# New lists for a set-attention kernel: loads after the first batch may be issued by either of two engines

## The chip, the cores and the metric

The kernel runs on one core of a Trainium2 chip. A core has five engines that work at the same time: TensorE (PE, matrix products, with a path of its own for loading weights, PEld), VectorE (DVE), ScalarE (ACT), GpSimd (POOL) and SyncE (SP), and sixteen DMA engines that move data between device memory and the core. The metric is the device time of the whole program in microseconds (us). Before the change it was 273.87 us, the median of three runs (273.7 to 274.29).

## What is computed

There are four batches of 12800 rows of 128 channels. First an attention through 32 inducing rows: the inducing rows attend to x, which gives h (32 rows), and then every row of x attends to h. On the result a gated product follows: a causal convolution of five taps over the rows, put through a sigmoid, times a linear map of the same rows, times an output matrix.

```python
def mab(q, kv):
    s = scale * (q @ kv.transpose(0, 2, 1))
    s = s - s.max(-1, keepdims=True)
    a = np.exp(s)
    a /= a.sum(-1, keepdims=True) + 1e-09
    return a @ kv
h = mab(I, x)                 # 32 inducing rows attend to 12800 rows of x
x = mab(x, h)                 # every row of x attends to the 32 rows of h
for k in range(5):
    gate_pre += conv_w[k] * xp[:, k:k + S, :]
out = (1 / (1 + exp(-gate_pre)) * (x @ w_val)) @ w_out
```

## The kernel before

The rows of a batch are cut into seven or eight chunks of up to 480 columns on each of four strips. Two copies of x are loaded: `xt` (channels on the partitions, `load_xt`, line 244), which both attentions score, and `xk` (rows on the partitions, `load_xk`, line 274), which the first attention sums. For most chunks of batch 0 there is no load of `xk`: PE transposes `xt` instead (line 298) and ACT or DVE copies the result (line 199). A full load is close to 1 MB.

The stages of a chunk are: scores of the inducing rows (`s1`, line 320) and their maximum (line 349), the exponential (ACT, line 366), the weighted sum h (`h`, line 398). When a batch has all its h, a short chain of small steps joins the groups (lines 415 to 466, DVE and PE), then come the scores of every row against h (`s2`, line 611) with a softmax over DVE, POOL and ACT (lines 617 to 691) that leaves `P`, the weights in two halves of float16. The matrix `W` (line 540, many small products with the identity, `ident`) folds h with the value matrix and the taps. For a block of rows the gate is PE's line 705 and the linear map line 714, ACT's sigmoid line 764, the product line 774 on DVE, its two halves lines 792 and 797, the output product line 823 and the store line 849.

Nothing of the order is left to a scheduler while the kernel runs. `Plan.op` records 1534 steps and numbers them. The list `SEQ` gives all of them in one order, and each engine follows it for its own steps; `BANKS` gives each accumulator one of four banks of PSUM; `ELSE` puts a step on another engine than its usual one. A transfer is issued by an engine's own instruction stream, so it stands in line behind that engine's earlier instructions. In the kernel before, loads of batches 0 and 1 are SP's (of batch 1 `ELSE` may put one on ACT) and those of batches 2 and 3 are ACT's.

Each buffer (`BUFS`: 11 of `xt`, 4 of `xk`) is taken by a new load once all readers of its former content are done. Transfers also share eight semaphores in turn: a transfer waits until an earlier one that used its semaphore has landed, in the lists of instructions the waits on `DMAHW0` to `DMAHW7`.

Of the kernel before, what the change touches and what calls it, by code (L numbers as in the profile page):

```python
# [26 lines left out]
SP = 1024.0  # L27
# [63 lines left out]
def tile_kernel(ctx: ExitStack, tc: tile.TileContext, xt, xk, indT_in, w64, out):  # L91
# [18 lines left out]
    op = plan.op  # L110
# [101 lines left out]
    blocks = []  # L212

    def load(dur, fn, new, use=(), b=0):
        return op("SP" if b < 2 else "ACT", dur, fn, [], new, use, dma=(dur, "load"), alt=dict(SP=dur, ACT=dur) if b == 1 else None)
# [663 lines left out]
    def ws():  # L879
        nonlocal iw  # L880
        iw = weights(load(0.66, f_wload, [("tg", "w", 0)]))
# [216 lines left out]
```

## Time and profile before

| | before |
|---|---|
| median of three runs | 273.87 us |
| the profiled execution | 274.29 us |
| its span in the trace | 272.3 us |
| PE busy in the span | 262.5 us, 96% |
| DVE, POOL, ACT busy | 229.0, 206.2, 198.2 us |
| moved by DMA | 75.49 MB, mean 277 GB/s |

The profiled execution took 274.29 us, of which 272.3 are the span between its first and last recorded work; 2.0 us lie around it. PE is the engine that is nearly always busy, so the time is PE's work and the moments at which PE stands still. DMA is nearly full in the first sixth of the run and has room later: over the span it moves 277 GB/s, in the first 45 us some 415.

The program itself is also read by DMA. The profile has a queue for it, with packets of about 16.5 KB. Where it says that an engine waited for "issue", the engine waited for nothing that the profile shows: no semaphore of another engine's work released it.

### The profile page before, as it was taken

What the parts mean: (1) busy time and instruction counts of PE and PEld (TensorE: products, weight loads), DVE (VectorE), ACT (ScalarE), POOL (GpSimd) and SP (SyncE); (2) the same over time, 40 slices, a digit from 0 to 9 for tenths busy, and PEclk for the clock granted to TensorE, in tenths of its full rate; (3) what the DMA queues carried; (4) which work ended last, traced back from release to release, by engine and by line L of the source; (5) the groups of instructions that cost most, each with busy time, mean ns of one, the idle gap of its engine ahead of it and who ended that gap; (6) DMA issues with size and microseconds to landing.
All of it is one profiled execution on the core that took longest, in us unless ns stands there. A gap on an engine that the chain in (4) does not pass through costs nothing.

```text
span 272.3 us, 11127 instructions
## 1 busy us (share of the span) xinstructions
PE 262.5 (96%) x4705; PEld 145.2 (53%) x4705; DVE 229.0 (84%) x539; ACT 198.2 (73%) x300; POOL 206.2 (76%) x233
## 2 busy tenths in 40 slices
PE   8999888999999999999999999999999999999984
PEld 3668436655665565485444455574544445444542
DVE  1678888899789999988899999879979999888842
ACT  2456157777877895877789788787788887777793
POOL 2000366878868979869899988888999999998960
PEclk9999999999999999999999999999999999999999
DMA  7999998898899989989999999734253323434547
GB/s 272 425 415 420 414 394 348 296 339 332 237 400 370 389 276 375 346 243 385 300 307 368 327 338 353 258 111 151 97 191 139 120 110 132 172 142 163 184 164 285
DMA packets 35377, 75.49 MB, mean 277 GB/s; under 512 B 2816, under 2 KB 26752, under 8 KB 35328
## 3 DMA queue, kind: packets, MB, share of 16 engines
q10 hardware_dynamic: 19520, 36.96, 39.1%
q1 hardware_dynamic: 15808, 37.82, 36.5%
q8 instruction: 37, 0.61, 0.9%
q14 instruction: 12, 0.10, 0.1%
HBM read 48.56 MB, written 26.21 MB: 275 GB/s over the span
## 4 chain that ended last, share of the span: by engine, by line
PE 95%; DVE 1%; issue 1%; ACT 1%; DVEq 0%; ACTq 0%
PE g L705 31%; PE a L823 24%; PE a L398 9%; PE a L611 8%; PE a L320 8%; PE a L714 6%; PE g L298 3%; PE a L859 1%; PE a L540 1%; PE a L813 1%; PE a L465 1%; ACT xk L199 0%; PE a L484 0%; PE a L349 0%; PE a L566 0%
## 5 line engine op out<-in xcount | busy, mean ns | idle before, releaser
L797 POOL TENSOR_TENSOR gl<-tg,gh 128x960 f16<-128x960 f32 (+4 forms) x54 | 101.2, 1878 | 12.3 <-ACT gh L792 6.5
L705 PE MATMUL g<-P,W 32*128 32x480 f16 (+4 forms) x1740 | 103.1, 345 | 1.3 <-issue 1.3
L705 PEld LDWEIGHTS <-W 32*128 32x128 f16 x1740 | 51.3, 92 | 42.7 <-issue 12.3
L774 DVE SCALAR_TENSOR_TENSOR tg<-tg,a 128x480 f32<-128x480 f32 (+4 forms) x116 | 65.4, 602 | 7.1 <-PE a L714 4.5
L792 ACT CAST gh<-tg 128x960 f16<-128x960 f32 (+4 forms) x54 | 50.1, 929 | 17.2 <-DVE tg L774 14.9
L823 PE MATMUL a<-gh,wo 128*32 128x480 f16 (+6 forms) x618 | 61.4, 348 | 0.8 <-DVE tg L774 0.7
L764 ACT ACTIVATE tg<-g,gsc 128x960 f32<-128x960 f32 (+4 forms) x58 | 55.7, 993 | 4.5 <-PE g L705 3.8
L823 PEld LDWEIGHTS <-wo 128*32 128x32 f16 (+1 forms) x939 | 35.2, 97 | 35.2 <-issue 14.2
L714 PE MATMUL a<-P,W 32*128 32x480 f16 (+4 forms) x348 | 41.9, 345 | 0.1
L836 DVE TENSOR_SCALAR os<-a,osc 128x480 f32<-128x480 f32 (+4 forms) x59 | 37.8, 661 | 4.8 <-PE a L823 3.8
L823 PE MATMUL a<-gl,wo 128*32 128x480 f16 (+6 forms) x309 | 41.5, 347 | 0.0
L838 ACT ACTIVATE os<-a,osc 128x448 f32<-128x448 f32 (+3 forms) x49 | 30.7, 638 | 5.9 <-PE a L823 3.2
L691 POOL TENSOR_TENSOR P<-pt,P 128x480 f16<-128x480 f32 (+4 forms) x29 | 30.1, 1037 | 4.1 <-ACT P L684 3.8
L398 PE MATMUL a<-xk,et 128*32 128x129 f32 x800 | 29.3, 274 | 0.2 <-issue 0.2
L628 POOL TENSOR_TENSOR e<-e,m 128x480 f32<-128x480 f32 (+4 forms) x29 | 27.2, 940 | 2.8 <-DVE m L622 1.9
L398 PEld LDWEIGHTS a<-xk,et 128*32 128x32 f32 x800 | 25.4, 110 | 6.4 <-issue 2.9
L611 PE MATMUL a<-xt,hT 128*32 128x480 f32 (+4 forms) x232 | 27.7, 541 | 0.1
L673 POOL TENSOR_TENSOR e<-e,z 128x480 f32<-128x480 f32 (+4 forms) x29 | 27.1, 937 | 0.6 <-DVE z L666 0.2
L320 PE MATMUL a<-xt,indT 128*32 128x480 f32 (+4 forms) x232 | 27.4, 544 | 0.2 <-DVE bt L172 0.2
L328 DVE TENSOR_SCALAR_CACHE_REDUCE ss<-a 128x480 f32<-128x480 f32 (+4 forms) x29 | 17.5, 605 | 7.2 <-PE a L320 6.8
L366 ACT ACTIVATE ss<-ss,ng 128x480 f32<-128x480 f32 (+4 forms) x29 | 18.0, 656 | 5.2 <-DVE ng L356 5.1
L684 ACT CAST P<-pt 128x480 f16<-128x480 f32 (+4 forms) x29 | 16.2, 561 | 7.5 <-DVE pt L679 7.0
(112 smaller groups left out, 285.4 us busy)
## 6 DMA issues: line engine op xcount, KB each, us to landing
xt<-in_xt_dram ACTq DMA_DIRECT2D x10, 960.0 KB, 7.3
out_dram<-os SPq DMA_DIRECT2D x35, 240.0 KB, 2.6
xk<-in_xk_dram ACTq DMA_DIRECT2D x8, 967.5 KB, 7.7
xt<-in_xt_dram SPq DMA_DIRECT2D x7, 960.0 KB, 10.2
out_dram<-os SPq DMA_DIRECT2D x28, 224.0 KB, 3.3
xk<-in_xk_dram ACTq DMA_DIRECT2D x6, 903.0 KB, 8.0
xk<-in_xk_dram SPq DMA_DIRECT2D x5, 903.0 KB, 12.5
out_dram<-os ACTq DMA_DIRECT2D x17, 240.0 KB, 3.7
```

The costliest lines, as they stand in the source:

```text
L320: T.matmul(s[32 * r:32 * r + 32, :n], c_["indT"], x[:, o:o + n // 32, r, :], start=True, stop=True)
L398: T.matmul(t[32 * s:32 * s + 32, :P + 1], st["et", b, c][:, 32 * i:32 * i + 32], st["xk", b, q][:, m + i, :], start=j < R, stop=j >= n - R)
L611: T.matmul(s[32 * r:32 * r + 32, :n], st["hT", b], x[:, m:m + nb, r, :], start=True, stop=True)
L705: T.matmul(st[f"g{r // 2}", b, c][:, r % 2, :n], st["W", b][q, w, k, :], st[("P1", "P2")[e]][q, o:o + n], start=u == 0, stop=u == len(taps ...
L714: T.matmul(st["a", "v", b, c, r][:, :n], st["W", b][q, w, TAPS, :], st[("P1", "P2")[e]][q, o:o + n], start=u == 0, stop=u == 2)
L764: S.activation(t[:, :, :n], st[f"g{p}", b, c][:, :, :n], AF.Tanh, scale=st["gsc", b])
L774: V.scalar_tensor_tensor(t, t, 1.0, st["a", "v", b, c, r][:, :n], ALU.add, ALU.mult)
L792: S.copy(sb(pw, g1, [P, 2, CW], F16)[:, :, :n], st[tg][:, :, :n])
L797: G.tensor_tensor(sb(pw, g2, [P, 2, CW], F16)[:, :, :n], st[tg][:, :, :n], st[g1][:, :, :n], ALU.subtract)
L823: T.matmul(t[o:o + wide], w[:, e, o:o + wide], st[g][:, q, :n], start=(e, g) == (0, g1), stop=g == g2)
L836: V.tensor_scalar(o, a, st["osc", b], None, ALU.mult)
L838: S.activation(o, a, AF.Copy, scale=st["osc", b])
```

## The change

Three things are changed: the rule by which a load gets its usual engine, and the three lists. The sets of steps, the stage functions, the buffers and the sizes stay as they are.

The rule: a load recorded before the first block of rows (`blocks` still empty) is SP's, any later one is ACT's, and `ELSE` may put any load from batch 1 on onto the other one of the two.

```diff
     def load(dur, fn, new, use=(), b=0):
-        return op("SP" if b < 2 else "ACT", dur, fn, [], new, use, dma=(dur, "load"), alt=dict(SP=dur, ACT=dur) if b == 1 else None)
+        return op("ACT" if blocks else "SP", dur, fn, [], new, use, dma=(dur, "load"), alt=dict(SP=dur, ACT=dur) if b else None)
...
 SEQ = [
-    5, 1, 15, 0, 12, 8, 18, 73, 36, 27, 2, 4, 39, 60, 3, 67, 6, 9, 30, 70, 86, 33, 7, 10, 16, 17, 11, 31, 32, 13, 74,
...
 ELSE = {
-    10: "DVE", 20: "DVE", 22: "ACT", 113: "ACT", 248: "ACT", 285: "DVE", 288: "ACT", 291: "ACT", 303: "DVE",
...
+    34: "DVE", 48: "ACT", 66: "ACT", 113: "ACT", 122: "ACT", 166: "ACT", 181: "ACT", 190: "ACT", 285: "DVE",
+    288: "SP", 296: "DVE", 297: "ACT", 306: "DVE", 328: "ACT", 334: "ACT", 369: "ACT", 394: "DVE", 407: "DVE",
+    408: "ACT", 410: "SP", 426: "ACT", 428: "SP", 447: "SP", 452: "ACT", 455: "ACT", 456: "ACT", 458: "DVE",
...
```

In the order of the program the numbers 86 and 109 are the two loads of `xk` of batch 0; 121, 181, 165 and 189 are `xt` of chunks 0 to 3 of batch 1; 122, 182, 166 and 190 are their `xk`; 287, 280, 291 and 409 are the next loads of `xt`.

The first place is SP, from the load of `xk` numbered 86 on, with the semaphores that each waits for. Before, the rows are 86, 109, 121, then three `xt` (181, 165, 189), then 166 and 122:

```order
L274 DMA xk<-in_xk_dram 128x1935 [waits DMAHW2_49]
L274 DMA xk<-in_xk_dram 128x1935 [waits DVE_49,PE_49,DMAHW3_49,Activation_49,Pool_49]
L244 DMA xt<-in_xt_dram 128x1920 [waits DMAHW4_49]
L244 DMA xt<-in_xt_dram 128x1792 [waits DMAHW5_49]
L244 DMA xt<-in_xt_dram 128x1792 [waits DMAHW6_49]
L244 DMA xt<-in_xt_dram 128x1792 [waits DMAHW7_49]
L274 DMA xk<-in_xk_dram 128x1806 [waits DMAHW2_49,DMAHW0_49,PE_49]
L274 DMA xk<-in_xk_dram 128x1806 [waits DVE_49,PE_49,DMAHW1_49,Activation_49,Pool_49]
```

After, the same stretch of SP is 86, 109, 121, two `xt` (165, 189) and 182, then stores:

```order
L274 DMA xk<-in_xk_dram 128x1935 [waits DMAHW2_49]
L274 DMA xk<-in_xk_dram 128x1935 [waits DMAHW3_49]
L244 DMA xt<-in_xt_dram 128x1920 [waits DMAHW4_49]
L244 DMA xt<-in_xt_dram 128x1792 [waits DMAHW5_49]
L244 DMA xt<-in_xt_dram 128x1792 [waits DMAHW7_49]
L274 DMA xk<-in_xk_dram 128x1806 [waits DVE_49,PE_49,DMAHW4_49,Activation_49,Pool_49]
L849 DMA out_dram<-os 128x128 [waits DMAHW0_49,Activation_49]
```

The load 109 no longer waits for PE, DVE, ACT and POOL (for the readers of a buffer that it takes over), only for an earlier transfer; it and 121, 165 and 189 behind it can so be issued as earlier ones land. The `xt` numbered 181 has left SP.

The second place is ACT, from the copies of h of batch 0 to the first sigmoid. Before, no transfer is issued there:

```order
L438 ACTIVATE H<-H,f 128x129
L199 COPY H<-a 128x129
L504 CAST w_516<-wf 128x160
L634 ACTIVATE e<-e 128x160
L559 ACTIVATE dq<-identf,q 128x128
L199 COPY W<-a 128x768
L634 ACTIVATE e<-e 128x320
```

After, four loads stand between ACT's steps up to that sigmoid (line 764), here 181, 122, 280 and 166 in this order:

```order
L199 COPY H<-a 128x129
L244 DMA xt<-in_xt_dram 128x1792
L504 CAST w_545<-wf 128x160
L559 ACTIVATE dq<-identf,q 128x128
L274 DMA xk<-in_xk_dram 128x1806
L634 ACTIVATE e<-e 128x160
L199 COPY W<-a 128x768
L634 ACTIVATE e<-e 128x320
L244 DMA xt<-in_xt_dram 128x4x448
L199 COPY W<-a 128x768
L684 CAST P_110<-pt 128x160
L274 DMA xk<-in_xk_dram 128x1806
```

What moved: loads that SP issued in close groups are now issued one at a time between ACT's copies and casts, and each leaves when ACT has come that far. In the other direction 18 loads of batches 2 and 3, all ACT's before, and one of batch 1 stand among SP's stores.

## Rows read from the trace of the kernel before

**Rows 1.** The page, parts 1 and 4: busy time by engine; the chain by engine.

```profile
PE 262.5 (96%) x4705; PEld 145.2 (53%) x4705; DVE 229.0 (84%) x539; ACT 198.2 (73%) x300; POOL 206.2 (76%) x233
PE 95%; DVE 1%; issue 1%; ACT 1%; DVEq 0%; ACTq 0%
```

**Rows 2.** PE's waits: engine, line, what released it, us in total, times, longest.

```profile
PE g L705 <- issue: 1.3, 2, 1.0
PE a L540 <- issue: 1.3, 1, 1.3
...
PE a L465 <- DVE cmax L187: 0.6, 1, 0.6
...
PE a L398 <- issue: 0.2, 1, 0.2
...
PE a L823 <- issue: 0.2, 1, 0.2
```

**Rows 3.** PE in order of time, 26 to 55: start, us, work, [idle before].

```profile
27.23 1.07 PE L398 MATMUL a<-xk,et 128*32 128x129 f32 x26 [0.17 <-issue]
...
36.43 0.23 PE L540 MATMUL a<-ident,w 128*32 128x128 f16 x2 [1.25 <-issue]
...
42.98 0.99 PE L705 MATMUL g<-P,W 32*128 32x320 f16 x21 [1.04 <-issue]
...
48.52 0.36 PE L705 MATMUL g<-P,W 32*128 32x480 f16 x1 [0.25 <-issue]
...
54.26 0.29 PE L823 MATMUL a<-gh,wo 128*32 128x128 f16 x5 [0.15 <-issue]
```

**Rows 4.** Stretches: PE, PEld, DVE, ACT, POOL busy (instructions), clock, DMA share, GB/s.

```profile
27.10:36.30 9.20, 7.21 (x126) 3.66 (x126) 7.85 (x33) 2.33 (x5) 4.19 (x10) 1.00 1.02 415
...
48.40:54.20 5.80, 5.59 (x128) 4.12 (x127) 4.83 (x12) 4.46 (x7) 4.80 (x7) 1.00 0.94 334
...
60.00:100.00 40.00, 40.00 (x801) 23.74 (x800) 36.43 (x89) 32.69 (x51) 33.17 (x36) 1.00 0.94 332
```

**Rows 5.** The page, part 3: packets, MB and share of the queue of instructions.

```profile
q8 instruction: 37, 0.61, 0.9%
```

**Rows 6.** SP in order of time: start, us to the last issue's end, issues.

```profile
5.55 12.03 SPq L274 DMA_DIRECT2D xk<-in_xk_dram  x2
17.63 1.85 SPq L244 DMA_DIRECT2D xt<-in_xt_dram  x4
24.71 1.96 SPq L274 DMA_DIRECT2D xk<-in_xk_dram  x2
```

**Rows 7.** Landing times; single issues at 2.6, 3.6, 17.3, 17.7, 18.2, 18.7, 19.2, 24.8.

```profile
xt<-in_xt_dram SPq DMA_DIRECT2D x1, 960.0 KB, 8.3
xt<-in_xt_dram SPq DMA_DIRECT2D x1, 960.0 KB, 12.0
xk<-in_xk_dram SPq DMA_DIRECT2D x1, 967.5 KB, 8.2
xt<-in_xt_dram SPq DMA_DIRECT2D x1, 960.0 KB, 10.2
xt<-in_xt_dram SPq DMA_DIRECT2D x1, 896.0 KB, 11.9
xt<-in_xt_dram SPq DMA_DIRECT2D x1, 896.0 KB, 13.7
xt<-in_xt_dram SPq DMA_DIRECT2D x1, 896.0 KB, 15.4
xk<-in_xk_dram SPq DMA_DIRECT2D x1, 903.0 KB, 11.9
```

**Rows 8.** POOL in order of time, at 40.5.

```profile
40.51 0.80 POOL L691 TENSOR_TENSOR P<-pt,P 128x320 f16<-128x320 f32 x1 [0.38 <-ACT P L684]
```

**Rows 9.** PE in order of time, 5 to 9: the same transposes twice.

```profile
5.28 1.54 PE L298 MATMUL g<-identf,xt 128*128 128x128 f32 x6
...
7.47 1.09 PE L298 MATMUL g<-identf,xt 128*128 128x128 f32 x8
```

More of the change, by code (lines that the diff above doesn't have):

```diff
@@ L956 @@
 SEQ = [
[71 rows of a table removed]
[71 rows of a table added]
 ]
 BANKS = (
-    "0123012301212312320123012301321321321021020123013201320132012301230210321032010310231023102310231021"
-    "3021032130230132102301301230213021320130213012032102301230123021302103213012301230120312032103213012"
-    "3102301230123012301321320130131023013203120310231231023012301203213203210231021302312013013021320132"
-    "01302130120321032103203120321032102310320320320312"
+    "0123012301300230031023102313203201302310313021301203102132032103210323012310210230132013201231021320"
@@ L1034 @@
+    "1320312032032102302130213012302310213123012013201320123021302130132013203213021302130213021302132103"
+    "2103120312031203123012101230203120312031032130213021301203102312013021302103103103210321302312031201"
+    "20321320310231023012312310321032102301103210321032"
 )
 ELSE = {
-    10: "DVE", 20: "DVE", 22: "ACT", 113: "ACT", 248: "ACT", 285: "DVE", 288: "ACT", 291: "ACT", 303: "DVE",
-    329: "ACT", 332: "ACT", 334: "ACT", 394: "DVE", 407: "DVE", 426: "ACT", 452: "ACT", 456: "ACT", 458: "DVE",
@@ L1038 @@
-    459: "ACT", 465: "ACT", 496: "ACT", 513: "ACT", 514: "ACT", 561: "ACT", 581: "ACT", 603: "DVE", 624: "ACT",
-    625: "ACT", 642: "DVE", 643: "ACT", 705: "ACT", 738: "ACT", 739: "ACT", 741: "DVE", 742: "ACT", 778: "ACT",
-    788: "ACT", 791: "DVE", 792: "ACT", 838: "ACT", 852: "ACT", 853: "ACT", 855: "DVE", 919: "DVE", 937: "ACT",
-    975: "ACT", 980: "ACT", 1001: "ACT", 1016: "ACT", 1019: "DVE", 1049: "ACT", 1056: "ACT", 1077: "DVE", 1078: "ACT",
-    1087: "ACT", 1114: "ACT", 1115: "ACT", 1140: "ACT", 1147: "ACT", 1153: "ACT", 1180: "ACT", 1181: "ACT",
@@ L1043 @@
-    1195: "DVE", 1199: "ACT", 1218: "DVE", 1220: "ACT", 1239: "ACT", 1253: "DVE", 1254: "ACT", 1287: "ACT",
-    1307: "ACT", 1332: "ACT", 1352: "ACT", 1355: "DVE", 1356: "ACT", 1389: "ACT", 1391: "DVE", 1415: "ACT",
-    1437: "ACT", 1445: "DVE", 1466: "ACT", 1467: "ACT", 1469: "ACT", 1470: "ACT", 1501: "DVE", 1509: "ACT",
-    1513: "ACT", 1518: "ACT", 1522: "SP", 1527: "DVE", 1530: "ACT", 1533: "SP",
+    34: "DVE", 48: "ACT", 66: "ACT", 113: "ACT", 122: "ACT", 166: "ACT", 181: "ACT", 190: "ACT", 285: "DVE",
@@ new lines @@
+    288: "SP", 296: "DVE", 297: "ACT", 306: "DVE", 328: "ACT", 334: "ACT", 369: "ACT", 394: "DVE", 407: "DVE",
+    408: "ACT", 410: "SP", 426: "ACT", 428: "SP", 447: "SP", 452: "ACT", 455: "ACT", 456: "ACT", 458: "DVE",
+    464: "DVE", 513: "ACT", 540: "DVE", 561: "ACT", 564: "ACT", 598: "SP", 621: "ACT", 625: "ACT", 626: "SP",
+    627: "SP", 630: "SP", 634: "SP", 639: "DVE", 642: "DVE", 646: "ACT", 648: "ACT", 704: "ACT", 732: "DVE",
+    733: "ACT", 736: "ACT", 739: "ACT", 778: "ACT", 783: "SP", 784: "SP", 788: "ACT", 792: "ACT", 828: "SP",
@@ new lines @@
+    832: "SP", 837: "ACT", 852: "ACT", 855: "DVE", 864: "DVE", 867: "ACT", 898: "SP", 899: "SP", 919: "DVE",
+    945: "SP", 946: "SP", 969: "SP", 970: "SP", 978: "ACT", 980: "ACT", 998: "ACT", 1016: "ACT", 1017: "ACT",
+    1042: "ACT", 1048: "ACT", 1055: "DVE", 1083: "ACT", 1087: "ACT", 1096: "ACT", 1114: "ACT", 1146: "ACT",
+    1149: "ACT", 1150: "ACT", 1178: "ACT", 1180: "ACT", 1198: "ACT", 1199: "ACT", 1218: "DVE", 1220: "ACT",
+    1254: "ACT", 1272: "ACT", 1287: "ACT", 1289: "DVE", 1290: "ACT", 1326: "ACT", 1331: "DVE", 1332: "ACT",
@@ L1047 @@
+    1349: "ACT", 1358: "ACT", 1391: "DVE", 1392: "ACT", 1394: "ACT", 1437: "ACT", 1439: "ACT", 1443: "ACT",
+    1445: "DVE", 1469: "ACT", 1470: "ACT", 1495: "ACT", 1498: "ACT", 1499: "ACT", 1501: "DVE", 1504: "DVE",
+    1509: "ACT", 1518: "ACT", 1521: "DVE", 1522: "SP", 1527: "DVE", 1530: "ACT", 1532: "DVE", 1533: "SP",
 }
```

141 rows, old and new, of the table SEQ are left out of this document.

## The prediction

> **What bounds the kernel now.** I read the busy shares and the chain first: PE works 262.5 of 272.3 us, and 95% of the chain that ends last is PE's own [rows 1]. What a new order can win or lose is therefore PE's idle time, and only that. So the next view is the list of PE's waits. Apart from the start and the end it holds 0.6 us for a step of DVE, and five waits released by "issue", by nothing that the profile shows: 1.3 (in two), 1.3, 0.2 and 0.2 us [rows 2]. In order of time they end at 27.23, 36.43, 42.98, 48.52 and 54.26, after 0.17, 1.25, 1.04, 0.25 and 0.15 us, 2.9 in all [rows 3].
>
> What are they? The reader should count instructions between them. Between the first and the second PE did 126 matmuls and PEld 126 weight loads, 252 together; between the last two 128 and 127, 255 [rows 4]. The whole program has 4705 of each, 9410, and the queue of instructions brought 37 packets: 254 a packet, 16.5 KB each [rows 1, 5]. So PE stops at the border of a packet of its own program that hasn't arrived. Nothing else spaces five waits in four different lines that evenly.
>
> Why does a packet come late? From 60 to 100 us PE runs through 801 matmuls, over six packets, and is busy 40.00 of 40.00 us, with DMA 0.94 full; it starved with DMA at 1.02 and also, between 48.4 and 54.2, at 0.94 [rows 4]. So the load on DMA alone doesn't tell the two apart; the depth of what is queued may. The issues with their landing times show it. Between 17.25 and 19.5 SP issued five loads, the first of them in the last 0.33 us of the group that ends at 17.58: 109 lands at 25.5 (17.25 + 8.2), then 27.8 (121), 30.0 (181), 32.3 (165) and 34.5 (189) [rows 6, 7], 2.2 to 2.3 us apart: that is what one load costs the full DMA. The wait that ends at 27.23 ends just under the landing of 121; the one that ends at 36.43 just under that of the load issued at 24.71, which lands at 36.6 [rows 3, 6, 7]. I read this as: a packet of instructions waits behind every load that was issued before it was asked for, and behind none issued later. The packet of 27.23 was behind 121 (issued 17.6) and ahead of 181 (issued 18.1), so it was asked for at about 18 us.
>
> **The change part by part.** No matmul is added or taken away; the change moves loads and reorders steps.
>
> 1. Loads 109, 121, 165, 189 go out earlier on SP. Before, SP sat from 5.55 to 17.25 on load 109, which waits for the readers of its buffer [rows 6]. Now it waits for an earlier transfer only: 109, 121, 165 and 189 each for the landing of a transfer eight places or so before, and the latest of these, for 189, is that of the load issued at 3.6, which lands at 15.6; that for 165 the one issued at 2.6, landed at 10.9 [rows 7]. So by 16 us all four are in the queue. They land no sooner, since DMA is full: the same order 109, 121, then 165 and 189 at 30.0 and 32.3, where 181 and 165 were. But the packet asked for at about 18 us now has two more loads ahead of it, 165 and 189. At 2.2 us each, PE's first wait ends at 27.23 + 4.4 = 31.6 instead of 27.23. The same matmuls of line 398 stand before it on PE, as no step of PE's before this border changes sides, so PE comes to it at the same 27.1. Cost: +4.4. From above, the packet may have to wait until 189 has landed whole and then be read: the wait of 36.43 ended 0.2 before a landing, that of 27.23 0.6 before; put at up to 1.5 after it, that is 33.8, +6.6. From below, one load ahead and not two: +2.2. I take the +4.4. What is queued behind PE's wait: the rest of h of batch 0, the chain of lines 415 to 466, all of `s2`; on SP the load 182, which waits for the last h of batch 0; on ACT the load 181, behind the copy of an h. No engine has other work to hide it: everything of batch 0 hangs on h.
>
> 2. The later waits. After that border, loads go out one at a time, between ACT's steps (181, 122, 280, 166), where SP sent two or four in a row. PE and ACT pass those points 4.4 us later, while DMA goes on: when PE resumes at 31.6, the only loads outstanding are 189 (landing at 32.3) and 181 at most, where before there were five. The next packets then have one or two loads ahead of them, 2.2 to 4.4 us, and PE takes 9.2 and 6.5 us for one packet's instructions in this part (27.1 to 36.3 [rows 4], 36.4 to 43.0 [rows 3]). So they come in time. Gain: 1.25 + 1.04 + 0.25 + 0.15 = 2.7 [rows 3]. From below: part of it is not PE's to have. The linear map of line 714 that follows needs `P`, whose low half POOL makes from 40.51 to 41.31 [rows 8], just ahead of the wait that ends at 42.98. A PE that comes 1.25 earlier may wait for POOL instead, which leaves 1.4. From above, nothing but the five waits is there to be won: 2.9. I take 2.7.
>
> 3. The rest of `SEQ`, `BANKS` and `ELSE`. PE was busy 40.00 of 40.00 from 60 on [rows 4], so there is nothing to win there; what an engine other than PE does hides under it. Loads of batches 2 and 3 that now stand among SP's stores wait for a store's turn, and DMA has room from then on. I take 0, with ±0.6, the one wait for DVE in PE's list [rows 2], gone or doubled.
>
> The sum: +4.4 − 2.7 + 0 = +1.7 on the profiled execution, 274.29 to 276.0. That execution is 0.42 above the median of 273.87; the forecast as a median is 275.6.
>
> [...]
>
> **The rivals.**
>
> A. Faster: the packets don't stand behind all loads issued before, or the packet at 27.23 is asked for before 165 is in the queue. Then step 1 costs nothing, and what the waits of 36 to 54 us come from is the close groups of loads issued just before them (24.71 to 26.67, [rows 6]), which are gone. Time: −2.7, 271.6 in the profiled execution, 271.2 as a median. For it: PE starved at a DMA share of 0.94 too. Against it: the first wait's end fits 121 and no other load. It decides if the packet was asked for before about 11 us. Reaching 2.9 and the wait for DVE: 270.4.
>
> B. No change: step 1 at its lower end, one load ahead (+2.2), and step 2 between its ends (−2): 273.7 to 274.4. For it: the bounds are there; against it: both 165 and 189 are issued by 16 us, well before 18.
>
> [...]
>
> **How the numbers follow.** Forecast (steps 1 to 3): 0.43; C: 0.12; B: 0.13; A: 0.32. The forecast's own range goes from 4.4 − 2.9 − 0.6 = +0.9 to 6.6 − 2.7 = +3.9, so from 274.8 to 277.8 as a median. The range over all cases is 271.0 to 278.2: A's time just inside the lower end, C's just inside the upper. What a measurement of this kernel can tell from no change is about 0.2%, 0.55 us. Slower are the forecast and C: 0.55. Same is B: 0.13. Faster is A: 0.32.
>
> **What the changed profile would show.** Step 1 is right if PE has one long wait released by "issue" in line 398, from 27.1 to about 31.6, and SP shows the issues of 109 to 189 before 16 us. It is wrong if that wait is under 1 us; then A holds. Step 2 is right if no wait by "issue" of over 0.3 us stands in lines 540 and 705 afterwards; it is wrong if one does, most of all behind the pair 280 and 166. [...] Step 3 is wrong if PE's list of waits has a new line with DVE, ACT or POOL as releaser after 60 us. The forecast as a whole fails if packets of instructions are not served in the order of asking, or are asked for much sooner than I read from one wait.

## The result and the profile after

The changed kernel took 276.07 us, the median of five runs (275.39 to 276.6), against 273.87 (273.39 to 274.29) in five runs of the kernel before on the same chip: a ratio of 1.007, interval 1.0051 to 1.0088. The forecast was 275.6. It is near the measured number by luck, for its working failed: the long wait on which it rested isn't in the trace. And the difference itself was not found again on two other chips (below).

The profiled execution took 276.6 us, its span is 274.7. The page's parts 1 and 4 for the changed kernel, answering to [rows 1]:

```profile
PE 263.3 (96%) x4696; PEld 147.0 (54%) x4696; DVE 223.9 (81%) x528; ACT 203.5 (74%) x311; POOL 206.7 (75%) x233
...
PE 86%; DVE 5%; DMA 3%; ACT 2%; issue 1%; POOL 1%; ACTq 0%; DVEq 0%
```

The same matmuls (a few records are missing in either trace) keep PE busy 0.8 us longer, and the chain, PE's own to 95% before, now passes through DVE and a load. The list of PE's waits, in the columns of [rows 2]:

```profile
PE g L705 <- POOL gl L797: 1.2, 1, 1.2
PE a L859 <- DVE warm L115: 1.2, 1, 1.2
PE a L611 <- issue: 0.8, 1, 0.8
PE a L320 <- DMA xt<-in_xt_dram: 0.8, 1, 0.8
PE a L823 <- DVE tg L774: 0.7, 1, 0.7
PE g L298 <- ACT xk L199: 0.7, 1, 0.7
PE a L465 <- DVE cmax L187: 0.7, 1, 0.7
PE a L398 <- issue: 0.6, 1, 0.6
PE a L611 <- DVE e L617: 0.3, 1, 0.3
```

There is a wait for a load that the kernel before has nowhere, a wait of 0.7 near the start where that kernel waits 0.2, and three waits in the place of the five of [rows 3]. In order of time, start, us, work and the idle time before:

```profile
26.09 2.62 PE L398 MATMUL a<-xk,et 128*32 128x129 f32 x82
...
36.70 0.59 PE L611 MATMUL a<-xt,hT 128*32 128x480 f32 x2 [0.83 <-issue]
...
49.17 0.38 PE L705 MATMUL g<-P,W 32*128 32x480 f16 x2 [1.20 <-POOL gl L797]
...
55.24 0.52 PE L398 MATMUL a<-xk,et 128*32 128x129 f32 x9 [0.58 <-issue]
...
100.76 0.96 PE L320 MATMUL a<-xt,indT 128*32 128x448 f32 x8 [0.78 <-DMA xt<-in_xt_dram]
```

The first row is the place at which a wait until 31.6 us was forecast: 82 matmuls of line 398 in a row, no idle time. The row at 49.17 names POOL, and a reader should look that step up before believing it:

```profile
47.52 0.67 POOL L797 TENSOR_TENSOR gl<-tg,gh 128x256 f16<-128x256 f32 x1
```

It ended at 48.19, a microsecond before PE went on. This too is a packet's border.

SP's issues, answering to [rows 6], and the landing times of the two loads at 10.9 and 15.6 us (165 and 189):

```profile
5.83 2.38 SPq L274 DMA_DIRECT2D xk<-in_xk_dram  x2
8.57 7.33 SPq L244 DMA_DIRECT2D xt<-in_xt_dram  x3
28.88 0.33 SPq L274 DMA_DIRECT2D xk<-in_xk_dram  x1
```

```profile
xt<-in_xt_dram SPq DMA_DIRECT2D x1, 896.0 KB, 19.2
xt<-in_xt_dram SPq DMA_DIRECT2D x1, 896.0 KB, 17.9
```

So the issues moved as forecast: 109 at 7.9, 121 at 8.6, 165 at 10.9, 189 at 15.6, landing at 25.5, 27.9, 30.1 and 33.5.

**The packets' own times.** The trace has a record of every packet of instructions, which none of the views lists. Beside the moments at which PE reaches the border of a block these records show three things that the forecast lacked. A block is 256 instructions of PE, weight loads and steps on semaphores included: between the borders that end the five waits of [rows 3] the trace has 256, 257, 255 and 257. Packet 2 or "the second" is here the second of the 37 records, and the block that it brings is numbered like it.

- From 188 to 233 us, where DMA has room (share 0.37 before, 0.36 after), packets 28 to 33 start within 0.7 us of the moment at which PE enters the block before theirs, in both traces. I take that moment as the one from which a packet can be asked for; by this reading one packet is on its way ahead.
- At the borders where PE starves it goes on 1.2 to 1.5 us after the packet has landed, and the packet itself takes 0.9 to 1.1 us. PE starves (stands still for want of instructions) where the packet's wait until its start and these 2.2 to 2.6 us are longer than PE's time for the block before, 5.2 to 8.3 us at these borders of the two traces.
- While DMA is full (share 0.97 from 25 to 60 us in both traces), the wait until the start is 1.5 to 4.5 us in most cases (in the stretch from 25 to 60 us mostly 2.5 to 4.5, one to two loads of 2.2 us) and now and then 5 to 7. In the changed kernel packet 2 could be asked for at 21.9 us and started at 25.04, 3.1 us later, ahead of the landings of 121, 165 and 189 (27.9, 30.1 and 33.5), which had been in the queue for 6 us and more when it was asked for. It did not wait for every load issued before it.

So a packet of instructions can pass loads that are queued. What sets the size of its wait these records don't say. Records of loads take 0.29 us per descriptor of 7.7 KB and 0.08 us per one of 1.9 KB. A usual wait of 3.4 us is thus, by estimate, some 12 of the one and over 40 of the other, not one number of descriptors.

**Where the time went in this execution.** I lined the two traces up by work done, each step of PE at its usual time. The changed kernel is 1.4 us behind from 7 to 16 us, 0.3 at 31, level at 47 (0.1 ahead), 1.3 behind from 56, 1.1 at 98, 2.0 from 102 on to the end. The 1.4 is the start: PE's transposes take 240 ns each until 8.7 us. That 0.3 of it is left at 31 us is read from the alignment, which compares two different orders of steps; no row says what made up the rest, and neither trace has a wait for a load between 14 and 31 us. Packet 4, for which the kernel before starved 1.0 us, comes in time, and packets 5 and 6 cost 0.9 and 0.4 more. Then comes the wait for the load `xt` of chunk 4 of batch 2, which is issued at 91.55 on SP, behind stores, and lands at 100.62.

The start in the trace of the changed kernel (10 transposes in 2.40 us, 240 ns each):

```profile
4.55 1.06 PE L298 MATMUL g<-identf,xt 128*128 128x128 f32 x4
6.29 2.40 PE L298 MATMUL g<-identf,xt 128*128 128x128 f32 x10 [0.68 <-ACT xk L199]
```

and the same program, in another execution (the run called third below; 128 ns each):

```profile
4.56 0.74 PE L298 MATMUL g<-identf,xt 128*128 128x128 f32 x4
6.38 1.28 PE L298 MATMUL g<-identf,xt 128*128 128x128 f32 x10 [1.08 <-DMA xt<-in_xt_dram]
```

In the run called again below, the rows are the same up to these ten, and the ten are fast (131 ns each):

```profile
4.55 1.06 PE L298 MATMUL g<-identf,xt 128*128 128x128 f32 x4
6.29 1.31 PE L298 MATMUL g<-identf,xt 128*128 128x128 f32 x10 [0.68 <-ACT xk L199]
```

I put this down to TensorE's clock. The trace also keeps the clock that was granted, stretch by stretch, as 0.50 or 1.00, and its first stretch at 1.00 begins at 10.37 us in the first trace of the changed kernel, at 6.12 in "again" and at 4.83 in "third"; it is 6.89 in the kernel before, between the two groups of [rows 9]. The slow transposes lie ahead of these moments, the fast ones behind them. Ahead of them the trace has no value, and the views print 1.00 there, so the lower clock at the start is read from the rows; "rise" here means the start of that first stretch. The late start is seen in PE's busy time: 263.3 us here, 261.1 and 260.8 in "again" and "third", with the same 4696 records. It isn't made up soon. The same scores of line 611 go on at 34.86 us here (the row after a wait of 0.31 for DVE) and at 33.75 in "third", which then waits 0.68 us for a load of `xt` at 36.20, where this execution has no such wait.

### The profile page after: what moved, and what is told of

Its sections match the earlier page's. It is cut to its first block, busy times and chain, and to the rows that moved or that the text cites. A ratio compares the mean times of both kernels' runs of the same rounds, so it can differ in the third digit from the quotient of the medians.

```text
span 274.7 us, 11136 instructions
## 1 busy us (share of the span) xinstructions
PE 263.3 (96%) x4696; PEld 147.0 (54%) x4696; DVE 223.9 (81%) x528; ACT 203.5 (74%) x311; POOL 206.7 (75%) x233
## 4 chain that ended last, share of the span: by engine, by line
PE 86%; DVE 5%; DMA 3%; ACT 2%; issue 1%; POOL 1%; ACTq 0%; DVEq 0%
PE g L705 28%; PE a L823 24%; PE a L320 7%; PE a L611 7%; PE a L398 7%; PE a L714 5%; PE g L298 4%; DMA xt<-in_xt_dram 3%; PE a L859 1%; PE a L813 1%; ACT xk L199 1%; DVE e L617 1%; DVE tg L774 1%; DVE ss L328 1%; PE a L540 1%
## 5 line engine op out<-in xcount | busy, mean ns | idle before, releaser
L823 PE MATMUL a<-gh,wo 128*32 128x480 f16 (+7 forms) x612 | 61.5, 348 | 0.7 <-DVE tg L774 0.7
L823 PEld LDWEIGHTS <-wo 128*32 128x32 f16 (+1 forms) x930 | 34.6, 97 | 36.0 <-issue 14.5
L823 PE MATMUL a<-gl,wo 128*32 128x480 f16 (+7 forms) x306 | 41.3, 347 | 0.0
L838 ACT ACTIVATE os<-a,osc 128x480 f32<-128x480 f32 (+4 forms) x58 | 35.6, 633 | 5.7 <-PE a L823 5.1
L836 DVE TENSOR_SCALAR os<-a,osc 128x480 f32<-128x480 f32 (+4 forms) x50 | 32.0, 663 | 5.9 <-PE a L823 5.6
L673 POOL TENSOR_TENSOR e<-e,z 128x480 f32<-128x480 f32 (+4 forms) x29 | 27.1, 936 | 7.6 <-DVE z L666 6.4
L398 PE MATMUL a<-xk,et 128*32 128x129 f32 x800 | 31.0, 274 | 0.6 <-issue 0.6
L320 PE MATMUL a<-xt,indT 128*32 128x480 f32 (+4 forms) x232 | 29.9, 554 | 0.8 <-DMA xt<-in_xt_dram 0.8
L611 PE MATMUL a<-xt,hT 128*32 128x480 f32 (+4 forms) x232 | 28.5, 540 | 1.1 <-issue 0.8
L398 PEld LDWEIGHTS a<-xk,et 128*32 128x32 f32 x800 | 26.2, 110 | 6.3 <-issue 1.8
```

Of the source, the lines that this page charges most:

```text
L320: T.matmul(s[32 * r:32 * r + 32, :n], c_["indT"], x[:, o:o + n // 32, r, :], start=True, stop=True)
L398: T.matmul(t[32 * s:32 * s + 32, :P + 1], st["et", b, c][:, 32 * i:32 * i + 32], st["xk", b, q][:, m + i, :], start=j < R, stop=j >= n - R)
L611: T.matmul(s[32 * r:32 * r + 32, :n], st["hT", b], x[:, m:m + nb, r, :], start=True, stop=True)
L823: T.matmul(t[o:o + wide], w[:, e, o:o + wide], st[g][:, q, :n], start=(e, g) == (0, g1), stop=g == g2)
L836: V.tensor_scalar(o, a, st["osc", b], None, ALU.mult)
L838: S.activation(o, a, AF.Copy, scale=st["osc", b])
```

## The experiments

The first four ran on a second chip, beside 28 runs of the kernel before there. "Chip" numbers count the chips of this study.

**a_swap: the late load earlier.** In `SEQ` the numbers 634 and 630, both SP's loads, change places.

```diff
-    ... 494, 634, 468, ... 509, 630, 498, ...
+    ... 494, 630, 468, ... 509, 634, 498, ...
```

> The changed kernel with two loads on SP exchanged: xt of chunk 4 of batch 2 (first needed at 99.7 us) takes the earlier place, issued near 87 us, and xt of chunk 3 (first needed at 104.4 us) the later one, near 91.5. Theory 1 (one of the two places where the change loses time is the wait of TensorE for that load at 99.7 to 100.8 us): the wait goes, about 1.0 us less than the changed kernel's 276.07, so 275.1, ratio to the kernel before 1.0045. Rival (the wait only shows a delay that another engine would impose next, POOL or DVE): 275.8 to 276.2, and a new wait stands at the same place.

Measured: ratio 1.0006 (0.9978 to 1.0035), profiled execution 273.32 us. The wait near 100 us is gone. But this trace differs from the changed kernel's from the first microseconds on, where the programs are the same: third packet after 3.4 us and not 6.8, ten transposes in 1.28 us and not 2.40. So the number can't be put down to the exchange, and the changed kernel was not run on this chip. This run turned the question: what differs between executions of one program?

**a_big and a_small: the size of descriptors.**

```diff
-PARTS = [(1, 1), (4, 3)]
+PARTS = [(1, 1), (1, 1)]        # a_big
...
-PARTS[(b, c) >= (1, 4)]
+PARTS[(b, c) >= (1, 0)]         # a_small, wherever it stands, also in the host's part
```

> The changed kernel with all loads in one piece per partition and engine row (descriptors of 7.0 to 7.7 KB also from chunk 4 of batch 1 on, where they were 1.8 to 2.6 KB). Bytes, order and issues are the same. Theory N (a packet of instructions waits for the descriptors that its DMA engine has taken up, a number): the waits between asking and arriving in the stretch after 45 us grow from 3 to 4 us to 8 us and more, TensorE starves at most packet borders up to 200 us, 10 us or more slower. Theory B (it waits for an amount of data, or for the rest of the load in progress): no change beyond 0.5 us. Theory O (my prediction's: it waits for every load issued before it is asked for): no change either, since the order of issues is the same.

> The changed kernel with the loads of chunks 0 to 3 of batch 1 too in the smaller pieces (four of 1.8 to 1.9 KB or three of 2.4 KB where one of 7.2 KB was). Theory N: the longest wait of a packet, 6.8 us from TensorE's entering the block at 27.6 to the packet's start at 34.4, falls to 4 us or less, and the idle time of TensorE at 35.3 to 36.7 (0.8 by the list of waits, 1.4 from matmul to matmul) goes: 0.8 to 1.4 us faster than the changed kernel, 274.7 to 275.3. Theories B and O: that wait stays at 6.8 us, and the time at 276 or, with 2% more time for each smaller piece, up to 0.4 above it.

Measured: a_big 1.0046 (1.0009 to 1.0084). Packets 7 to 14, whose neighbours now are descriptors four times as large, waited 3.0 us in the mean, against 2.0 in the changed kernel's first trace (2.6 and 2.7 in its two later ones), and not 8: theory N is out. a_small 1.0097 (1.0063 to 1.013); its third packet waited 7.0 us among small descriptors, so N fails here too. Its waits of PE:

```profile
36.90 0.59 PE L611 MATMUL a<-xt,hT 128*32 128x480 f32 x2 [1.10 <-issue]
43.57 0.99 PE L705 MATMUL g<-P,W 32*128 32x320 f16 x22 [0.53 <-issue]
49.65 0.38 PE L705 MATMUL g<-P,W 32*128 32x480 f16 x2 [0.92 <-issue]
55.99 0.52 PE L398 MATMUL a<-xk,et 128*32 128x129 f32 x9 [0.85 <-issue]
```

Four borders, four starvings. The waits of both runs agree with theory B. Whether small pieces for four loads cost time isn't shown: the interval of a_small overlaps those of a_big and a_start, and the changed kernel was not run on this chip. a_small also has the late rise of the clock (10.23 us; ten transposes in 2.39 us).

**a_start: the start of the kernel before** (first 129 steps of its list, with their banks and engines).

```diff
-    5, 15, 12, 8, 73, 1, 4, 2, ...            # first 129 steps as changed
+    5, 1, 15, 0, 12, 8, 18, 73, 36, 27, ...   # first 129 as before, 165 behind 121
```

> The changed kernel with the order, banks and engines of the kernel before in the first 129 steps of the list (up to about 27 us; the load of xt of chunk 2 of batch 1 stays with its changed place beside the one of chunk 0). TensorE was 1.4 us behind the kernel before from 7 to 16 us in the changed kernel, by the work done. Theory 1 (that is made up by 47 us, since loads and packets bound the stretch behind it): within 0.4 us of 276.07. Rival (it is carried to the end): 274.7. Theory O for packets: with xt of chunk 3 of batch 1 issued later, the packets up to 43 us come earlier by up to 2 us; theories N and B: they don't.

Measured: 1.0071 (1.0039 to 1.0104), profiled execution 275.07. No gain against the 276.07 of the first chip (its median is 276.36), as theory 1 had it. Packets 2 and 3 waited 3.7 and 6.7 us, nearly as in the kernel before, though 189 was issued at 18.3 and not at 15.6: against theory O again.

**again: the changed kernel on a third chip** (no edit), with 23 runs of the kernel before.

> The changed kernel once more, unaltered, on the chip of the next three runs. In the exchange of two loads the same first 80 us of program gave other waits for packets than the changed kernel's first trace (third packet: 3.4 us from TensorE's entering the block to the packet's start, where it was 6.8). Theory 1 (the wait of a packet varies from execution to execution, the order of the loads doesn't set it): the third packet again waits 3 to 7 us, and the waits by issue up to 60 us add up to another sum than 1.4; the wait for a load near 100 us stands as before. Theory O (my prediction's: it waits for every load issued before it is asked for): 6.8 us again. Time: 1.005 to 1.009 of the kernel before.

Measured: 0.9997 (0.9964 to 1.0029), twelve runs from 272.73 to 279.31; the medians of all runs, 275.12 against 274.43, give 1.0025. The third packet waited 3.5 us, not 6.8: theory O is out on the one place where it had fitted best. Another packet was late instead, at a place where the traces of the changed kernel and of the kernel before have no wait (a_big has one of 0.91 there); the only row with idle time of PE between 121 and 126 us:

```profile
124.77 1.51 PE L705 MATMUL g<-P,W 32*128 32x448 f16 x28 [1.68 <-issue]
```

Packet 17 waited 5.3 us there, and by work done this execution falls from 0.8 ahead of the kernel before to 1.05 behind it at that row, and keeps it.

**b_loads and a_loads: loads of the one kernel in the order of the other.** All loads are taken out of `SEQ` and put in again behind the same step of PE as in the other kernel, with its engine.

```diff
-    ... 132, 158, ... 162, 181, 165, 135, 169, 136, 189, ...   # before
+    ... 121, 165, ... 189, ... 182, ...                        # b_loads: loads as changed
```

> The kernel before in the order of all other steps, banks and engines, with the loads alone placed and given to SP or ACT as in the changed kernel (behind the same step of TensorE; three moved up so as to precede their first reader). Theory 1 (the loss is of the loads: the late load near 100 us and what its neighbours cost): 1.004 to 1.008 of the kernel before, and a wait for a load near 100 us. Rival (the loss is of the new order of the other steps): 0.998 to 1.002.

> The counterpart: the changed kernel's order of all other steps with the loads placed and given to SP or ACT as in the kernel before. Theory 1 (the loss is of the loads): 0.998 to 1.003 of the kernel before, no wait for a load after 60 us. Rival (the order of the other steps): 1.004 to 1.009.

Measured: 1.124 (1.117 to 1.131) and 1.0358 (1.0311 to 1.0404), and both expectations fail. PE's longest waits, b_loads first:

```profile
PE a L320 <- DMA xt<-in_xt_dram: 21.1, 8, 6.0
PE a L398 <- DMA xk<-in_xk_dram: 8.4, 1, 8.4
```

```profile
PE a L320 <- DMA xt<-in_xt_dram: 6.4, 1, 6.4
```

The order of PE's steps and the order of loads are fitted to each other, so that "the loads alone" isn't a part that can be exchanged. These two runs tell nothing on where the 0.7% comes from. They do show what went with a long wait. In a_loads PE stood still for 6.43 us up to 99.09; the granted clock was 0.50 from 95.5 to 102.3 us, and the eight matmuls of line 320 behind the wait took 1.83 us, where eight of that size take about 1.0 in the other traces. In b_loads the mean granted clock was 0.946, and behind its waits of 6.00 and 8.40 us eight matmuls of line 320 took 1.83 us and 26 of line 398 took 1.72, where 26 take 0.94 to 1.07 elsewhere. No wait of the other traces is longer than 1.7 us, and there the clock stayed at 1.00 from its rise to the last 4 us.

**a_split: two transfers for one.** Each load of batches 1 to 3 is issued as two.

```diff
+    def both(b, dst, src):
+        ...
+        for i in range(2):
+            ...
+            issue().dma_start(dst[:, a:z], src[:, a:z])
...
-            issue().dma_start(st[key][:, first:first + n // 32]...
+            both(b, st[key][:, first:first + n // 32]...
```

> The changed kernel with every load of batches 1 to 3 issued as two transfers of half the bytes, one right behind the other on the same engine; the same bytes. What is open is the unit behind which a packet of instructions waits: neither larger nor smaller descriptors changed the waits of 2 to 4 us (about one and a half loads of 2.2 us). Theory T (it waits for the rest of the transfer in progress and one more that is taken up): the waits between TensorE's entering a block and the packet's start fall to 1 to 2 us in the stretch from 30 to 66 us, the waits by issue go, 1 to 2 us faster than the changed kernel. Theory B (an amount of bytes is taken up, whatever the transfers): the waits stay at 2 to 4 us; the time is that of the changed kernel or up to 1.5 us more, for twice the issues (0.4 us each on ACT) and since eight transfers in flight are now half as many bytes.

Measured: 1.003 (0.9998 to 1.0063) beside 0.9997 for the changed kernel on that chip. Packets 3 to 8 waited 3.5, 2.3, 3.5, 3.8, 2.9 and 2.7 us, 3.1 in the mean, against 3.4 in the run "again": theory T is out. This trace starves at one border only, for 0.69 us.

The last four ran on a fourth chip, beside 35 runs of the kernel before.

**third: the changed kernel once more.**

> The changed kernel a third time, beside the next three. On its first chip it took 1.0051 to 1.0088 of the kernel before, on a second one 0.9964 to 1.0029. Theory 1 (its waits for packets and the start differ from execution to execution; the lists make no steady difference of over 0.5%): between the two, 0.998 to 1.006, single executions spread over 3 us or more. Theory O (a steady wait that the lists cause): 1.005 to 1.009 again.

Measured: 0.9997 (0.9975 to 1.0019), 273.87 to 276.02, against 273.55 to 276.63 for the kernel before. Rows with idle time of PE from 30 to 60 us:

```profile
33.75 1.01 PE L611 MATMUL a<-xt,hT 128*32 128x480 f32 x8 [0.31 <-DVE e L617]
36.20 0.96 PE L320 MATMUL a<-xt,indT 128*32 128x448 f32 x8 [0.68 <-DMA xt<-in_xt_dram]
42.22 0.99 PE L705 MATMUL g<-P,W 32*128 32x320 f16 x22 [1.39 <-issue]
48.57 0.38 PE L705 MATMUL g<-P,W 32*128 32x480 f16 x2 [1.20 <-issue]
```

Here it is the fourth packet that came late (6.1 us), and the border at 48.57, where the first trace named POOL, names issue. The wait for the late load is there too, under another name: in the list of waits

```profile
PE a L320 <- DVE tg L774: 0.9, 1, 0.9
```

ends at 99.73 us, and the load of `xt` issued at 90.18 landed at 99.6.

**swap_again: the exchange beside it** (the edit of a_swap).

> The exchange of the two loads on SP (xt of chunks 4 and 3 of batch 2) once more, now beside the changed kernel on the same chip. If the wait for the load near 100 us is a steady loss: 0.003 to 0.004 below the changed kernel's ratio of the same chip. If it only stands where the start was slow or packets came otherwise: within 0.002 of it.

Measured: 0.9993 (0.9963 to 1.0024), within 0.0004 of the run "third". The exchange gains nothing that can be seen on this chip; with these intervals a gain of 0.3% isn't excluded. Without the exchange the wait near 100 us is in five traces of eight (0.78 in the first, 1.00 in a_small, 0.88 in third, 1.06 in a_warm, 0.47 in a_big; not in again, a_start and a_split, of which the last waits 0.69 at 107 us instead), and with it in none of three. So the exchange takes the wait away, and the time doesn't follow. On the second chip a_swap (up to 1.0035) lies below a_start (from 1.0039) and a_small (from 1.0063) and overlaps a_big; but these differ from it by more than the exchange, and the changed kernel itself is missing beside them. This trace has the late rise of the clock too (10.17 us).

**a_warm: PE held back by 1.7 us.**

```diff
-WARM = 8
+WARM = 12
```

> The changed kernel with twelve warm-up matmuls in place of eight, which keeps TensorE from its first real work for 1.7 us more (0.43 us each). In nine traces the third packet came 3.4 to 3.7 us after it could be asked for where TensorE entered that block at 26.4 us, and 6.7 to 7.0 us after where it entered at 27.2 to 27.6. Theory R (the moment decides: a packet that is asked for some 0.8 us later misses a place between the loads and comes a further stretch of loads later): TensorE enters at 27.0 or later, the wait is 6 us or more, and TensorE starves for over 1 us near 35 us. Rival (the two values belong to chips or executions, not to the moment): 3.4 to 3.7 where the changed kernel of the same chip has it. Time: up to 1.5 us above the changed kernel of this chip, or none where the start is bound by loads.

Measured: 0.9983 (0.9961 to 1.0006). PE entered the block at 27.1 us and the third packet started 3.0 us later; in swap_again PE entered at 27.47 and the packet waited 3.6. So theory R fails with the moments that it named. A limit just behind is not excluded: the three traces of changed versions that entered later (27.49 in a_start, whose first loads differ, 27.51 in a_small, 27.56 in the first trace) all waited 6.7 to 7.0. The 1.7 us cost nothing; PE starves twice up to 60 us in this trace:

```profile
46.70 0.38 PE L705 MATMUL g<-P,W 32*128 32x480 f16 x2 [0.96 <-issue]
...
53.05 0.53 PE L398 MATMUL a<-xk,et 128*32 128x129 f32 x11 [0.86 <-issue]
```

**swap_split: the exchange and the split.**

> The exchange of the two loads, with every load of batches 1 to 3 as two transfers of half the bytes: the version that lost least to packets in its trace (0.9 us of starving, 2.4 to 4.4 in the others) with the earlier load. If the fewer waits of that trace were of the transfers' size: 0.003 or more below the changed kernel of the same chip, at or under the kernel before. If they were chance: the ratio of the exchange alone, or up to 0.004 above it for the added issues.

Measured: 1.0046 (1.0025 to 1.0066), just above the exchange alone (up to 1.0024). So the split gains nothing, and the good trace of a_split is put down to chance. It costs 0.5% here and 0.3% on the third chip, where the intervals overlap; that the added issues are what costs is likely and not shown. No version here beats both kernels beyond its interval.

What single profiled executions show beside each other. All times are in us; those of packets are from their records. "Starved" is the sum of PE's idle times, as the rows give them, at the borders of packets; measured from matmul to matmul, as in the expectation of swap_split, the sums are larger (0.9 for a_split). "Clock" is the moment from which the trace has the granted clock at 1.00:

| execution | chip | time | clock | 3rd packet waited | 4th | starved |
|---|---|---|---|---|---|---|
| before | 1 | 274.29 | 6.9 | 6.8 | 4.1 | 2.9 |
| changed | 1 | 276.6 | 10.4 | 6.8 | 2.8 | 2.6 |
| changed (again) | 3 | 275.65 | 6.1 | 3.5 | 4.4 | 3.5 |
| changed (third) | 4 | 275.76 | 4.8 | 3.5 | 6.1 | 2.6 |
| a_swap | 2 | 273.32 | 4.7 | 3.4 | 2.7 | 1.7 |
| swap_again | 4 | 275.56 | 10.2 | 3.6 | 5.1 | 3.0 |
| a_warm | 4 | 274.55 | 7.0 | 3.0 | 2.5 | 1.8 |
| a_split | 3 | 274.0 | 4.5 | 3.5 | 2.3 | 0.7 |

## Why the prediction was right in number and wrong in its reasons

**Right:** that five of PE's waits are borders of packets (the trace gives 255 to 257 instructions between them, and the forecast's 254 leaves out 62 recorded steps of PE on semaphores); that no wait by issue is a fault of an engine; that the changed SP issues 109 to 189 before 16 us. The forecast of 0.6% near the measured 0.7% is luck, as the terms below show.

**Wrong, the premise.** "What a new order can win or lose is therefore PE's idle time, and only that." PE's own work took 0.8 us more than before in the first trace, and 2.2 to 2.5 more than in the two later traces of the same program, in which the clock rose sooner (6.12 and 4.83 us, against 10.37).

**Wrong, step 1 (+4.4).** "A packet of instructions waits behind every load that was issued before it was asked for." The trace shows packet 2 passing three loads; the term measured 0, as no wait stands there, and the 0.2 of [rows 3] at 27.23 went as well. The reading rested on two waits that ended just under a landing. With a landing every 2.2 us, some end of a wait always falls near one. And the moment of asking, 18 us, was inferred from that same fit; it is PE's entering the block before, 21.0 us in the kernel before.

**Wrong, step 2 (−2.7).** The waits did not go. In the first trace of the changed kernel three of 0.83, 1.20 and 0.58 us stand up to 60 us, 2.6 together, against 2.9 before [rows 3]: −0.3. In the three traces of the unaltered changed kernel PE starved 2.6, 3.5 and 2.6 us in all, against 2.9 in the one of the kernel before. The step took fewer loads outstanding for a shorter wait. But packets 4 to 6 waited 2.7 to 6.1 us in these three traces, and between 40 and 55 us, where PE is through with a block in some 5 to 6.5 us, a wait of 3.5 us or more starved it in six cases of seven.

**Wrong, step 3 (0).** It held the 1.4 us at the start and the wait for a load near 100 us, the two places where the first trace lies furthest behind. The bound of ±0.6 was too narrow: it counted one wait of the trace and no load that might come late on an engine with stores ahead of it. Its sign of being wrong named DVE, ACT and POOL, and the new line names a load. That neither loss is steady was seen only in the repeated runs.

So +1.7 was met by +2.3 from other terms: a late clock, a late load and packets late at other places. Of the rivals, A had the mechanism (packets don't stand behind all loads), with the wrong consequence, since the waits it let vanish are not made by the close groups of loads; B, no change, is what two chips of three show, though not by its reasons. The upper end of the range, 278.2, rests on C's time, 278.1, which adds 2.5 us for work of PE at half its rate behind a long wait. No run shows that term: the long wait isn't in the trace, and in a_loads, behind one of 6.43 us, eight matmuls took 1.83 us and not 1.0.

**What stays open.** Why the first chip gave 1.0051 to 1.0088 with five tight runs on either side, and the other two 0.9964 to 1.0029 and 0.9975 to 1.0019, is not settled. Its one trace of the changed kernel has the late clock, three late packets and the late load at once; whether that chip does so in most executions was not tried. Nor is it known why the clock rises late in some executions. And what makes a packet wait 6 to 7 us in one execution and 3.4 in another, with the same program up to that point, was not found: it isn't the order of issues alone (6.8 and 3.5 with the same lists), the size of descriptors (7.0 with small ones) or the moment of asking as theory R had it. The size of a transfer was tried only where the wait was short.

## What to carry to other kernels

In this kernel PE's program came by DMA, as its data did, in 37 packets of some 16 KB and, as read here, one packet ahead. While loads kept DMA full (share 0.97 from 25 to 60 us), it took mostly 4 to 7 us from PE's entering a block until it could go on with the next; where PE was through with the 256 instructions of a block sooner it starved at the border (0.15 to 1.25 us in the kernel before, 0.58 to 1.20 in the first trace after), and none of the orders of loads tried here prevented that. Before a wait's end is matched to a landing, ask how often it would match by chance, and look for a second execution of the same program. A difference of 0.7% on one chip, in a kernel whose single executions spread over 1% on others, is a result of that chip until it is repeated.

## What was not expected of the hardware

- PE's transposes after the same warm-up ran at 240 ns each until 8.7 us in one execution and at 131 ns from 6.3 us in another of the same program: the granted clock is on record, at 1.00, from 10.37 us in the one and from 6.12 in the other, after the same rows of work. The views' column of granted clock says 1.00 in both, as it does where the trace has no value.
- Twelve executions of an unaltered program lay between 272.7 and 279.3 us on one chip, and five between 275.4 and 276.6 on another.
- Twelve warm-up matmuls in place of eight, 1.7 us of added work ahead of everything, cost no time that can be measured (0.9983, interval 0.9961 to 1.0006). PE enters the block of packet 2 only 0.7 us later than in the run "third" (27.14 against 26.45), and has no wait at 36 us, where "third" waits 0.68 for a load.
